# Seven products for batch 0's second expert layer, with partial sums begun in PSUM by ScalarE

## The chip, the cores and the metric

The kernel runs on one core of a Trainium2 chip. The metric is the device time of one execution in microseconds. Without the change it is 1115.46 us, the median of 3 runs (1114.99 to 1116.11). About 0.2% can be told from no change.

## The reference, cut to what matters

Three parts follow each other on 4 batches of 576 tokens: an attention over 32 memory slots, a two-layer network with a leaky activation, and a mixture of 4 experts. The change lies in the last part, which is

```
x: [2304, 512]   w1: [4, 512, 1024]   w2: [4, 1024, 512]
p = domain_probs / (sum of domain_probs over experts + 1e-9)
for e in range(4):
    h = max(x @ w1[e], 0)
    out += p[:, e:e+1] * (h @ w2[e])
```

## The kernel before, in words

**Arithmetic.** All matrices are kept transposed: features on the 128 partitions, tokens along the free dimension, 288 tokens (HB, half a batch) to a matmul. Operands are split into a high part (ScalarE casts to fp32r) and a low part (VectorE or GpSimd subtracts, `sub_to`, line 309); a product takes three passes, high x high, high x low, low x high. So one block product with an inner length of 256 is 2 x 3 = 6 matmuls of 128x128 by 128x288.

**Units.** The experts' 4 x 1024 hidden features are 8 groups g of 512. `plan_experts` (line 1112) walks through units (half, g, b): first batches 0 and 1 for all g, then batches 2 and 3 for all g. In a unit, each of two parts hp (256 hidden features) is an `Up` (line 875): the first product by Strassen's algorithm in Winograd's form, 7 block products p1 to p7 (42 matmuls) into three PSUM banks ux, uy, uw out of the six of ps_a. p2 adds onto p1's bank, p7 and p4 onto p6's, p3 onto p5's. v1 copies p1's sum to SBUF, and VectorE adds it: v16 = uy + v1 after p6, v167 = uy + v1 after p7, and c21, c22 and c12 add in the bank or to SBUF. Batches 0 and 1 ("banked") are gated straight out of the banks (max with 0, times p; line 950); batches 2 and 3 are first written to h and then gated in halves (`gate_half`, line 966).

**Second product.** It runs as a side stream, one block at a time between the Ups of the next unit, into two banks (ps_h). `Down` (line 998) is plain: 8 blocks of 12 matmuls. `Seven` (line 1038) does it with seven products in two halves: 14 blocks of 6 matmuls, 4 differences S of the gated hidden features, 7 high parts H, 7 low parts L. Batch 0 uses Down for all 8 groups; batches 1 to 3 use Seven for g = 0 to 6 and Down for g = 7. After each block D, a flush F takes it to an accumulator in SBUF: a ScalarE copy for g = 0, a VectorE addition later. At the end of a batch the seven accumulators are combined (cb) and Down's last blocks are added and stored.

**Weights.** w1's sums (ws), high (wh) and low parts (wl) and w2's quarters (vh, vl), their four sums (ss, sh, sl) are made in the first half, stored to HBM (wk, vk, sk) and read again in the second half (wr, cl, vr), all by DMAs issued from SP's queue. The tiles of w2 lie in a ring of 8 (ring2), and one more, wP4, lies in another pool.

**The order.** Each of these steps is a named task. The string ORDER (line 30) lists them in the order in which they are issued; each engine runs its own instructions in that order and waits by semaphores for the others. The set ON_VECTOR (line 254) names the low parts, differences and sums that VectorE does; the others go to GpSimd. Names are kind, g, b, then hp or a number: p6_320 is p6 of group 3, batch 2, part 0; D32_5 a block of the second product.

Of the kernel before, what the change touches and what calls it, by code (L numbers as in the profile page):

```python
# [100 lines left out]
p5_100 c12_011 ws11 p6_100 wh11 sk0S1 D01_4 F01_4 D01_0 F01_0 S01_4 H01_4 sh0S4 p5_110 S01_5 H01_3 rw22 D01_3 F01_3
D01_5 wl110 wl111 F01_5 rw23 ss1S1 v16_100 p2_100 vh110 vh111 sl0S4 sk0S2 vk010 sk0S4 L01_4 p7_100 H01_5 S01_6 H01_6
p5_101 v167_100 c11_100 c22_100 D01_8 D01_9 p5_111 F01_8 p3_100 c12_100 F01_9 p1_101 p4_100 c21_100 vh101 ss1S2 sh1S1
p6_101 v1_101 v16_101 vl110 D01_2 F01_2 L01_5 D01_11 sl1S1 p7_101 L01_6 F01_11 v167_101 wk11 p2_101 hi0_100 D01_10
L01_3 D01_12 F01_12 p4_101 rw14 F01_10 ss1S4 sh1S4 vl111 vk011 D01_13 F01_13 p1_110 c11_101 c22_101 p6_110 hi1_100
c21_101 hi1_101 lo1_100 p3_101 c12_101 D01_7 p1_111 v1_110 p2_110 v16_110 lo0_100 vl101 p7_110 c11_110 D01_6 v167_110
hi0_101 rw15 sl1S4 F01_6 p4_110 wk10 F01_7 lo0_101 vh100 lo1_101 D10_4 c22_110 p3_110 c21_110 H11_0 F10_4 c12_110
vl100 ss1S3 D10_7 vk111 L11_0 ws20 S11_1 H11_1 L11_1 sh1S3 F10_7 pg11 D10_6 F10_6 p6_111 v1_111 v16_111 D11_1 F11_1
D10_0 F10_0 p2_111 c11_111 p7_111 v167_111 c22_111 D10_1 wh20 wl201 rw24 sl1S3 F10_1 wl200 p4_111 c21_111 D10_5 F10_5
p3_111 ws21 c12_111 S11_4 S11_5 wh21 D10_2 F10_2 p1_200 v1_200 pg10 wl211 D10_3 H11_2 L11_2 sk1S4 p6_200 F10_3 p5_200  # L110
D11_3 H11_3 p2_200 rw25 ss2S1 v16_200 F11_3 L11_3 wl210 p7_200 v167_200 H11_4 D11_5 sk1S1 H11_5 sk1S3 c11_200 vh200
vl200 vk110 L11_4 S11_6 p6_201 p4_200 c21_200 p1_201 v1_201 sh1S2 D11_9 F11_5 F11_9 sl1S2 p1_210 D11_4 sh2S1 sl2S1
D11_2 p5_211 c22_200 p3_200 F11_2 F11_4 D11_8 c12_200 F11_8 D11_0 F11_0 v16_201 p2_201 ss2S2 sh2S2 sl2S2 p5_201 vh201
p7_201 c11_201 v167_201 c22_201 H11_6 vk200 L11_5 D11_11 F11_11 hi1_200 ss2S3 p6_211 lo1_200 D11_6 F11_6 p4_201 D11_7
F11_7 L11_6 vl201 hi0_200 lo0_200 p3_201 c21_201 c12_201 D11_10 v1_210 hi1_201 lo1_201 vk100 p6_210 v16_210 wk20 rw16
D11_13 F11_13 F11_10 p5_210 vh210 p7_210 v167_210 p2_210 c11_210 c22_210 p4_210 c21_210 D11_12 vh211 p3_210 c12_210
hi0_201 vl211 lo0_201 sk1S2 F11_12 H21_0 p1_211 vk211 sk2S1 vl210 D20_3 vk210 F20_3 D20_6 wk21 L21_0 S21_1 F20_6
v1_211 v16_211 sk2S2 D20_0 F20_0 p2_211 c11_211 ws30 wh30 p7_211 v167_211 wl301 D20_2 H21_1 c22_211 p3_211 c12_211
D20_4 F20_4 wl300 sh2S3 sl2S3 L21_1 ss2S4 F20_2 p4_211 c21_211 rw17 ws31 D20_1 F20_1 D20_5 F20_5 D20_7 sh2S4 D21_0
S21_4 p1_300 F20_7 H21_3 L21_3 wk30 F21_0 wh31 wl310 D21_3 D21_2 rw27 vh311 v1_300 p2_300 F21_3 H21_2 H21_4 wl311  # L120
sl2S4 S21_5 c11_300 p6_300 v16_300 D21_1 F21_1 p5_300 rw26 ss3S1 L21_4 H21_5 D21_6 F21_2 F21_6 sk2S4 L21_2 p7_300
p6_301 D21_8 D21_4 L21_5 F21_8 D21_5 v167_300 p4_300 S21_6 F21_4 H21_6 c22_300 p3_300 rw18 F21_5 c21_300 L21_6 c12_300
D21_7 vh310 wk31 sh3S1 vl310 vk310 p1_301 F21_7 v1_301 v16_301 hi0_300 D21_9 lo0_300 p2_301 F21_9 hi1_300 sl3S1 D21_10
p7_301 p1_310 p5_301 v167_301 c11_301 c22_301 vh301 F21_10 vh300 vl300 D21_11 F21_11 p3_301 vk300 vl311 c12_301
lo1_300 p4_301 D21_12 c21_301 F21_12 D21_13 p6_310 F21_13 v1_310 p2_310 v16_310 c11_310 vk311 ss3S2 ss3S4 p7_310
v167_310 vl301 hi0_301 lo0_301 ws40 p5_310 c22_310 p4_310 p3_310 c21_310 hi1_301 lo1_301 p1_311 H31_0 v1_311 D30_3
L31_0 c12_310 wh40 D30_5 wl400 F30_5 sh3S2 sl3S2 F30_3 p6_311 wl401 p2_311 D30_2 F30_2 D30_1 v16_311 F30_1 rw19 ws41
sh3S4 S31_1 D31_0 p5_311 p7_311 c11_311 v167_311 c22_311 D30_0 F30_0 H31_1 L31_1 F31_0 p3_311 p4_311 D31_1 pg20
c12_311 c21_311 F31_1 sk3S1 wh41 wl410 D30_4 ss3S3 F30_4 p1_400 S31_4 sk2S3 sl3S4 D30_7 p6_400 F30_7 v1_400 v16_400
D30_6 wl411 sk3S2 D31_2 H31_2 L31_2 p7_400 S31_5 H31_5 rw28 H31_4 F30_6 v167_400 sh3S3 sl3S3 rw29 ss4S1 ss4S2 p6_401  # L130
L31_4 S31_6 D31_5 sh4S1 L31_5 F31_5 p5_400 p2_400 D31_3 c11_400 c22_400 p4_400 F31_2 p3_400 c21_400 H31_3 vh410 F31_3
vh400 vl400 wk40 D31_4 p1_401 rw111 F31_4 sl4S1 sk4S1 p6_410 pg21 c12_400 v1_401 p2_401 v16_401 hi1_400 vl410 L31_3
p7_401 D31_11 p1_410 hi0_400 vh411 F31_11 D31_9 H31_6 L31_6 lo1_400 v167_401 D31_8 vl411 F31_8 p4_401 c21_401 F31_9
sk3S3 D31_10 p5_401 vh401 F31_10 c11_401 ss4S4 c22_401 hi1_401 p5_410 D31_6 F31_6 v1_410 p3_401 c12_401 D31_7 p6_411
p2_410 v16_410 p7_410 lo1_401 F31_7 vl401 D31_13 D31_12 p1_411 v167_410 p4_410 c11_410 c22_410 sh4S4 hi0_401 lo0_401
lo0_400 F31_12 sl4S4 c21_410 p3_410 ss4S3 wk41 D40_0 H41_0 F31_13 D40_4 F40_0 D40_3 v1_411 p2_411 rw110 c12_410
# [137 lines left out]
def memory_attention_experts(ctx: ExitStack, tc: tile.TileContext, phi, q, kv, w_in, w_out, w1, w2, alpha, dp, out):  # L274
# [1335 lines left out]
```

## Time and profile before

| | |
|---|---|
| median of 3 runs | 1115.46 us |
| the profiled execution | 1115.43 us |
| its span, first to last instruction | 1113.3 us |
| TensorE, VectorE, ScalarE, GpSimd busy | 1105.6, 806.9, 443.6, 605.0 us |

The span is shorter than the execution by what lies around the program. In the rows, PE is TensorE's matmul and PEld its weight load, DVE is VectorE, ACT is ScalarE, POOL is GpSimd, SP is the queue that issues the DMAs; L888 is line 888 of the kernel. TensorE's matmuls overlap, so that a duration (296 ns) is longer than the distance between two starts.

### The profile page before, as it was taken

How to read it: one execution, taken by the hardware profiler on the slowest of the kernel's cores; microseconds unless marked ns; L12 is line 12 of the kernel's file. 1: busy time of each engine (PE TensorE's matmuls, PEld its weight loads, DVE VectorE, ACT ScalarE, POOL GpSimd, SP SyncE). 2: the span in 40 equal slices, each digit the busy share in tenths (PEclk: the TensorE clock that was granted, in tenths of full speed). 3: DMA queues.
4: the chain of work that ended last, by engine and by line, in shares of the span. 5: the costliest groups of instructions: out<-in, count | busy, mean ns of one | idle time of the engine just before them, and what ended most of it. 6: DMA issues, size and time to landing. Idle time of an engine off the chain costs nothing.

```text
span 1113.3 us, 21930 instructions
## 1 busy us (share of the span) xinstructions
PE 1105.6 (99%) x8668; PEld 1071.8 (96%) x8668; DVE 806.9 (72%) x1570; ACT 443.6 (40%) x911; POOL 605.0 (54%) x487
## 2 busy tenths in 40 slices
PE   9999999999999999999999999999999999999998
PEld 8679999999999999999999999999999999999998
DVE  6987786767556767777877777846677777777786
ACT  5676654534444544333333234324522222223220
POOL 3666555522345587898788878774433333335500
PEclk9999999999999999999999999999999999999999
DMA  9930211211020427585557364686555554634702
GB/s 371 390 145 21 95 58 58 76 40 40 1 87 30 181 96 295 178 312 202 190 230 267 116 257 156 232 319 203 178 176 177 180 162 154 218 126 149 253 7 85
DMA packets 61046, 181.20 MB, mean 163 GB/s; under 512 B 6288, under 2 KB 23696, under 8 KB 57232
## 3 DMA queue, kind: packets, MB, share of 16 engines
q1 hardware_dynamic: 60944, 179.80, 45.2%
q8 instruction: 68, 1.11, 0.4%
q14 instruction: 34, 0.28, 0.1%
HBM read 115.52 MB, written 64.26 MB: 161 GB/s over the span
## 4 chain that ended last, share of the span: by engine, by line
PE 97%; DVE 2%; issue 0%; ACT 0%; POOL 0%; POOLq 0%; DVEq 0%
PE c L1083 20%; PE y L690 17%; PE uy L888 14%; PE o L1015 13%; PE uw L888 9%; PE ux L888 9%; PE h L656 9%; PE y L687 1%; PE pw L615 1%; PE warm L322 1%; PE pm L424 1%; PE h L653 1%; PE pc L456 0%; DVE w L309 0%; DVE h L1058 0%
## 5 line engine op out<-in xcount | busy, mean ns | idle before, releaser
L690 PE MATMUL y<-g,wout 128*128 128x288 f32 x1440 | 205.3, 296 | 0.0
L690 PEld LDWEIGHTS y<-g,wout 128*128 128x128 f32 x1440 | 195.3, 188 | 7.3 <-ACT g L675 2.5
L888 PE MATMUL uy<-x,w 128*128 128x288 f32 x1152 | 183.7, 296 | 0.0
L309 POOL TENSOR_TENSOR gc<-h,gc 128x576 fp32r<-128x576 f32 x78 | 117.6, 1514 | 119.5 <-ACT gc L1066 119.4
L888 PEld LDWEIGHTS uy<-x,w 128*128 128x128 f32 x1152 | 162.7, 188 | 0.7 <-DVE v L922 0.5
L1066 ACT CAST gc<-h 128x576 fp32r<-128x576 f32 x119 | 79.3, 675 | 196.6 <-DVE h L1058 121.5
L1083 PE MATMUL c<-gc,w2c 128*128 128x288 f32 x1008 | 155.0, 295 | 0.5 <-DVE acc2y L1101 0.5
L1083 PEld LDWEIGHTS c<-gc,w2c 128*128 128x128 f32 x1008 | 140.7, 188 | 0.8 <-DVE acc2y L1101 0.8
L309 POOL TENSOR_TENSOR g<-act,g 128x288 fp32r<-128x288 f32 x80 | 68.5, 864 | 125.5 <-ACT g L675 84.1
L888 PE MATMUL uw<-x,w 128*128 128x288 f32 x768 | 122.4, 296 | 0.2 <-DVE ux L922 0.2
L1015 PE MATMUL o<-g,w 128*128 128x288 f32 x864 | 122.4, 295 | 0.0
L888 PE MATMUL ux<-x,w 128*128 128x288 f32 x768 | 122.2, 295 | 0.0
L1015 PEld LDWEIGHTS o<-g,w 128*128 128x128 f32 x864 | 117.1, 188 | 0.0
L656 PE MATMUL h<-a,wp 128*128 128x288 f32 x720 | 110.2, 296 | 0.0
L671 DVE SCALAR_TENSOR_TENSOR act<-neg,bet,h 128x288 f32<-128x288 f32 x120 | 60.4, 510 | 67.9 <-ACT neg L662 62.2
L888 PEld LDWEIGHTS uw<-x,w 128*128 128x128 f32 x768 | 108.5, 188 | 0.5 <-DVE ux L922 0.4
L888 PEld LDWEIGHTS ux<-x,w 128*128 128x128 f32 x768 | 108.8, 188 | 0.0
L656 PEld LDWEIGHTS h<-a,wp 128*128 128x128 f32 x720 | 99.9, 188 | 5.7 <-issue 2.3
L662 ACT ACTIVATE neg<-h 128x288 f32<-128x288 f32 x128 | 52.2, 411 | 97.6 <-PE h L656 94.9
L1101 DVE TENSOR_TENSOR acc<-c,acc 128x288 f32<-128x288 f32 x144 | 64.9, 454 | 35.4 <-PE c L1083 33.3
L922 DVE TENSOR_TENSOR v<-uy,v 128x288 f32<-128x288 f32 x128 | 58.1, 454 | 40.2 <-PE uy L888 36.9
L675 ACT CAST g<-act 128x288 fp32r<-128x288 f32 x120 | 51.2, 433 | 43.7 <-DVE act L671 32.9
(195 smaller groups left out, 1832.9 us busy)
## 6 DMA issues: line engine op xcount, KB each, us to landing
kw<-w SPq DMA_DIRECT2D x16, 1792.0 KB, 8.9
raww<-in_w SPq DMA_DIRECT2D x32, 512.0 KB, 4.7
w<-kw SPq DMA_DIRECT2D x32, 512.0 KB, 4.8
kS<-sS SPq DMA_DIRECT2D x28, 512.0 KB, 5.8
w2c<-kS SPq DMA_DIRECT2D x28, 512.0 KB, 4.5
kw<-w SPq DMA_DIRECT2D x25, 512.0 KB, 5.5
w<-kw SPq DMA_DIRECT2D x48, 256.0 KB, 4.3
kv<-in_kv SPq DMA_DIRECT2D x8, 1152.0 KB, 12.3
```

What stands on the lines that cost most here:

```text
L309: eng.tensor_tensor(out=out, in0=in0, in1=in1.bitcast(F32), op=ALU.subtract)
L656: mm(p, wp_t[b, c, g][:, x, fs], a_t[b][:, y, g, o:o + HB], start=(n == 0), stop=(n == 5))
L662: nc.scalar.activation(out=self.neg, in_=self.p, func=AF.Relu, scale=-1.0)
L671: nc.vector.scalar_tensor_tensor(out=self.g, in0=self.neg, scalar=bet[:, ft:ft + 1], in1=self.p, op0=ALU.mult, op1=ALU.add)
L675: nc.scalar.copy(out=self.gt[:, 0, 0:HB], in_=self.g)
L690: mm(First.acc[d], w[:, x, d * 128:(d + 1) * 128], self.gt[:, y, 0:HB], start=(self.start and n == 0), stop=(self.stop and n == 2))
L888: mm(p, w[:, x, a, k], operand(self.b, i)[:, y, k], start=(start and n == 0), stop=(n == 5), skip_group_check=not start)
L922: nc.vector.tensor_tensor(out=out, in0=x, in1=y, op=ALU.add)
L1015: mm(p, w[:, x, i, d % 2 * 128:(d % 2 + 1) * 128], g, start=(m == 0), stop=(m == 11), skip_group_check=len(hps) == 1)
L1066: nc.scalar.copy(out=t[:, 0], in_=self.raw(q))
L1083: mm(p, w[:, x, i, m * 128:(m + 1) * 128], self.g_t[q][:, y, i], start=(k == 0), stop=(k == 5))
L1101: nc.vector.tensor_tensor(out=a, in0=self.ps[n], in1=a, op=ALU.add)
```

## The change

Batch 0 is done like batch 1: Seven for g = 0 to 6, Down for g = 7. In all Ups, v1 copies p1's sum from ux into the bank uy before p6, and p6, p7 and p4 add onto it; v16 and v167 become ScalarE copies of uy, and c21 is gated straight from uy. All batches are gated from the banks, so that the half gates go. For b < 2 and g > 0, every odd block n of Seven is "seeded": a new task E copies the accumulator into the block's bank on ScalarE, the product adds onto it, and the flush is a ScalarE copy. A first matmul with `start=True` in uy, whose result is overwritten by v1, is added to each p1 of group 0 and batch 0. c21's, v16's and v167's additions go.

The differences, the sums of w1 and w2 and the low parts of w2 can now be on either engine (`engine(...)`), and ON_VECTOR grows from 280 to 426 names. ring2 has 7 buffers for 8, the pool yt 9 for 6, and wP4 goes into ring2. The pieces of w2 are made at other places of a group's two units, and quarter (0, 1) is made for g = 7 alone. ORDER is new from its 1271st task on (the last tasks of the layer before); it has 4247 tasks for 4080.

The core of the diff, without ORDER and ON_VECTOR:

```diff
-        for name, key, bufs in (("w1b", ("w1", 1), 1), ("pp", "p", 2), ("hp", "h", 3), ("vp", "v", 1), ("ring2", "w2", 8), ("accp", "acc", 2), ("yt", "y", 6), ("xt", "xt", 2)):
+        for name, key, bufs in (("w1b", ("w1", 1), 1), ("pp", "p", 2), ("hp", "h", 3), ("vp", "v", 1), ("ring2", "w2", 7), ("accp", "acc", 2), ("yt", "y", 9), ("xt", "xt", 2)):
...
+        t = pools["w2"].tile([128, 2, 512], F32R, tag="w", name=f"w2c{g}{q}")
...
+    def seeded(g, b, n):
+        return g > 0 and b < 2 and n % 2 == 1
...
-            self.seven, self.hs = b > 0 and g < NG - 1, None
-            self.banked = b < 2
+            self.seven, self.hs = g < NG - 1, None
...
         def p1(self):
             self.x = self.bank("ux")
             self.product(self.x, A11, B11, True)
+            if (self.g, self.b) == (0, 0):
+                self.y = self.bank("uy")
+                w = w1_t[self.g, self.hp].rearrange("p x (c k n) -> p x c k n", c=7, k=2)
+                mm(self.y, w[:, 0, A11, 0], operand(self.b, B11)[:, 0, 0], start=True, stop=True)
 
         def p6(self):
-            self.y = self.bank("uy")
-            self.product(self.y, V2, T2, True)
+            self.product(self.y, V2, T2, False)
...
         def v1(self):
-            self.v1_t = self.v("v1")
-            nc.scalar.copy(out=self.v1_t, in_=self.x)
+            if (self.g, self.b) != (0, 0):
+                self.y = self.bank("uy")
+            nc.scalar.copy(out=self.y, in_=self.x)
 
         def v16(self):
             self.v16_t = self.v("v16")
-            self.add(self.v16_t, self.y, self.v1_t)
+            nc.scalar.copy(out=self.v16_t, in_=self.y)
...
         def c11(self):
-            if self.banked:
-                self.gated(0, 0, self.x)
-            else:
-                nc.scalar.copy(out=self.block(0, 0), in_=self.x)
+            self.gated(0, 0, self.x)
...
         def added(self, i, j, bank, x, y):
-            if self.banked:
-                self.add(bank, x, y)
-                self.gated(i, j, bank)
-            else:
-                self.add(self.block(i, j), x, y)
+            self.add(bank, x, y)
+            self.gated(i, j, bank)
...
         def v167(self):
             self.v167_t = self.v("v167")
-            self.add(self.v167_t, self.y, self.v1_t)
+            nc.scalar.copy(out=self.v167_t, in_=self.y)
...
         def c21(self):
-            self.added(1, 0, self.y, self.y, self.v1_t)
+            self.gated(1, 0, self.y)
...
-            if not self.late and q in (P1, P2, P4):
+            if n not in self.ps:
+                self.ps[n] = ps_h.tile([128, 512], F32, tag="h", name=f"c{self.name}{n}")[:, 0:HB]
+            p, fresh = self.ps[n], not seeded(self.g, self.b, n)
+            if self.b < 2 and q in (P1, P2, P4):
                 w = w2_t[(self.g,) + C_W[q]]
             else:
...
-                    mm(p, w[:, x, i, m * 128:(m + 1) * 128], self.g_t[q][:, y, i], start=(k == 0), stop=(k == 5))
+                    mm(p, w[:, x, i, m * 128:(m + 1) * 128], self.g_t[q][:, y, i], start=(fresh and k == 0), stop=(k == 5), skip_group_check=not fresh)
                     k += 1
+
+        def seed(self, n):
+            q, m = divmod(n, 2)
+            p = self.ps[n] = ps_h.tile([128, 512], F32, tag="h", name=f"c{self.name}{n}")[:, 0:HB]
+            nc.scalar.copy(out=p, in_=acc_t[self.b][q][:, m])
...
             a = acc_t[b][q][:, m]
-            if self.g == 0:
+            if self.g == 0 or seeded(self.g, b, n):
                 nc.scalar.copy(out=a, in_=self.ps[n])
             else:
                 nc.vector.tensor_tensor(out=a, in0=self.ps[n], in1=a, op=ALU.add)
...
+                if g == NG - 1:
+                    if t == 0:
+                        more.setdefault((1, 1), []).extend((do_w2, g, hp, 0) for hp in range(2))
+                        more.setdefault((1, 3), []).extend((do_w2, g, hp, 1) for hp in range(2))
+                else:
                     for place, fs in (
-                        ((1, 1), [(do_sum, g, "S1")]),
-                        ((1, 2), [(do_part, g, "S1", 0), (do_sum, g, "S2")]),
-                        ((1, 3), [(do_part, g, "S1", 1), (do_part, g, "S2", 0)]),
-                        ((1, 4), [(do_sum, g, "S4"), (do_part, g, "S2", 1)]),
+                        ((0, 3), [(do_w2, g, 0, 0)]),
+                        ((0, 4), [(do_sum, g, "S1")]),
+                        ((1, 0), [(do_part, g, "S1", 0), (do_sum, g, "S2")]),
+                        ((1, 1), [(do_w2, g, 1, 0), (do_part, g, "S1", 1)]),
+                        ((1, 2), [(do_sum, g, "S4"), (do_part, g, "S4", 0)]),
+                        ((1, 3), [(do_part, g, "S4", 1), (do_sum, g, "S3"), (do_raw, 4 * g + 4)]),
+                        ((1, 4), [(do_part, g, "S3", 0)]),
...
+                        ((0, 0), [(do_part, g, "S3", 1), (do_part, g, "S2", 0)]),
+                        ((0, 1), [(do_part, g, "S2", 1), (do_w2, g, 1, 1)]),
...
-                    loads = {-1: [(do_c_load, 0, q) for q in (P1, P5, P4)], 3: [(do_c_load, 0, q) for q in (P2, P3)], 7: [(do_c_load, 0, q) for q in (P7, P6)]}
+                    loads = {-1: [(do_c_load, 0, q) for q in (P1, P5, P4)], 7: [(do_c_load, 0, q) for q in (P2, P3, P7, P6)]}
...
+                more.setdefault((0, 4), []).extend((do_unspill, 2, i, j) for i, j in ((0, 0), (0, 1), (1, 1)))
...
                     do(f"D{old.g}{old.b}_{n}", old.product, n)
+                    if old_seven and n < 13 and seeded(old.g, old.b, n + 1):
+                        do(f"E{old.g}{old.b}_{n + 1}", old.seed, n + 1)
                     do(f"F{old.g}{old.b}_{n}", old.flush, n)
```

## Rows read from the trace of the kernel before

**Rows 1.** Busy time, share and instructions of each engine, whole span, from the page.

```profile
PE 1105.6 (99%) x8668; PEld 1071.8 (96%) x8668; DVE 806.9 (72%) x1570; ACT 443.6 (40%) x911; POOL 605.0 (54%) x487
```

**Rows 2.** Chain that ended last, shares of the span by engine, from the page.

```profile
PE 97%; DVE 2%; issue 0%; ACT 0%; POOL 0%; POOLq 0%; DVEq 0%
```

**Rows 3.** Stretches: start:end, length, busy (instructions) by engine, granted clock, DMA share, GB/s.

```profile
372.00:745.00 373.00, 372.41 (x2792) 370.88 (x2791) 278.07 (x524) 139.49 (x244) 298.87 (x227) 1.00 0.60 222
745.00:1110.00 365.00, 364.46 (x2747) 364.00 (x2745) 263.52 (x512) 104.89 (x201) 125.78 (x83) 1.00 0.48 160
812.00:1005.00 193.00, 193.00 (x1458) 193.00 (x1458) 145.78 (x296) 52.51 (x95) 64.21 (x43) 1.00 0.54 176
```

**Rows 4.** Groups by line, tile and shape: xcount, busy us, mean ns, idle before. Plain second product.

```profile
L1015 PE MATMUL o<-g,w 128*128 128x288 f32 x864 | 122.4, 295 | 0.0
...
L1015 PE MATMUL o<-g,w2l 128*128 128x288 f32 x192 | 26.1, 295 | 0.0
```

**Rows 5.** Timeline around one Up of batch 2: start us, duration us, engine, line.

```profile
905.27 0.96 PE L888 MATMUL ux<-x,w 128*128 128x288 f32 x6
...
905.94 0.85 PEld L1083 LDWEIGHTS c<-gc,w2c 128*128 128x128 f32 x6
906.07 0.95 PE L1083 MATMUL c<-gc,w2c 128*128 128x288 f32 x6
906.27 0.40 ACT L926 COPY v<-ux 128x288 f32<-128x288 f32 x1 [0.87 <-PE ux L888]
906.74 0.84 PEld L888 LDWEIGHTS uy<-x,w 128*128 128x128 f32 x6
906.86 0.95 PE L888 MATMUL uy<-x,w 128*128 128x288 f32 x6
```

**Rows 6.** Timeline where a sum v16 came late, first half; idle time in brackets.

```profile
416.04 2.88 DVE L309 TENSOR_TENSOR w<-s,w 128x1024 fp32r<-128x1024 f32 x1
...
418.21 0.86 PEld L888 LDWEIGHTS ux<-x,w 128*128 128x128 f32 x6
...
418.85 0.45 DVE L922 TENSOR_TENSOR v<-uy,v 128x288 f32<-128x288 f32 x1
...
419.35 0.83 PEld L888 LDWEIGHTS uy<-x,w 128*128 128x128 f32 x6 [0.28 <-DVE v L922]
```

**Rows 7.** Groups of VectorE in the first half, 372 to 745 us.

```profile
L922 DVE TENSOR_TENSOR v<-uy,v 128x288 f32<-128x288 f32 x66 | 29.9, 453 | 17.6 <-PE uy L888 14.9 <-ACT g L991 1.0 <-PE c L1083 0.8
...
L1032 DVE TENSOR_TENSOR acc<-o,acc 128x288 f32<-128x288 f32 x56 | 24.8, 453 | 21.1 <-PE o L1015 20.9
...
L309 DVE TENSOR_TENSOR gc<-h,gc 128x576 fp32r<-128x576 f32 x21 | 19.9, 950 | 3.0 <-ACT gc L1066 3.0
L309 DVE TENSOR_TENSOR w<-s,w 128x1024 fp32r<-128x1024 f32 x11 | 18.4, 1671 | 2.0 <-ACT w L793 2.0
L309 DVE TENSOR_TENSOR g<-h,g 128x576 fp32r<-128x576 f32 x14 | 16.6, 1183 | 1.7 <-ACT g L991 1.6
...
L309 DVE TENSOR_TENSOR sS<-S,sS 128x512 fp32r<-128x512 f32 x12 | 12.1, 1008 | 0.0
```

**Rows 8.** Groups of VectorE in the second half, 745 to 1110 us.

```profile
L968 DVE SCALAR_TENSOR_TENSOR c<-c,p 128x576 f32<-128x576 f32 x28 | 21.5, 767 | 1.8 <-ACT c L948 0.7
...
L309 DVE TENSOR_TENSOR gc<-h,gc 128x576 fp32r<-128x576 f32 x20 | 15.9, 797 | 0.0
```

**Rows 9.** Groups of ScalarE over the whole span.

```profile
L1066 ACT CAST gc<-h 128x576 fp32r<-128x576 f32 x119 | 79.3, 675 | 196.6 <-DVE h L1058 121.5 <-POOL h L1058 21.6 <-PE o L1015 12.8
...
L926 ACT COPY v<-ux 128x288 f32<-128x288 f32 x64 | 25.5, 398 | 65.1 <-PE ux L888 43.2 <-DVE uy L922 15.7 <-DVE uw L922 2.6
...
L1099 ACT COPY acc<-c 128x288 f32<-128x288 f32 x24 | 9.5, 402 | 12.1 <-PE c L1083 12.0
```

**Rows 10.** Transfers of w2's weights: xcount, size, median us from issue to landing.

```profile
w2c<-kw SPq DMA_DIRECT2D x14, 512.0 KB, 5.8
```

More of the change, by code (lines that the diff above doesn't have):

```diff
@@ L826, in s_sum @@
         x, y = (cs_t[g, i] if i in ("S1", "S2") else a[i] for i in (x, y))
-        nc.gpsimd.tensor_tensor(out=o, in0=x, in1=y, op=op)
+        engine(f"ss{g}{n}").tensor_tensor(out=o, in0=x, in1=y, op=op)
     def s_hi(g, n):
@@ L934, in open @@
                 return
-            if self.seven and self.hp and b_late(self.b):
-                if not c_raw:
-                    for j in range(2):
-                        c_raw[j] = rawp.tile([128, 1024], F32, tag="raw", name=f"c{j}")[:, 0:S].rearrange("p (i n) -> p i n", i=2)
-                self.hs = c_raw
-            else:
-                self.h = pools["h"].tile([128, 4, HB], F32, tag="h", name="h" + self.name)
-                self.hs = [self.h[:, 2 * j:2 * j + 2] for j in range(2)]
+            self.h = pools["h"].tile([128, 4, HB], F32, tag="h", name="h" + self.name)
+            self.hs = [self.h[:, 2 * j:2 * j + 2] for j in range(2)]
         def c11(self):
-            if self.banked:
-                self.gated(0, 0, self.x)
-            else:
-                nc.scalar.copy(out=self.block(0, 0), in_=self.x)
+            self.gated(0, 0, self.x)
         def gated(self, i, j, src):
@@ L1061, in hi @@
             k = self.slot[q]
[L1062 to L1065 removed]
+            c = self.b // 2, k // 2
+            if c not in c_slot:
+                c_slot[c] = unit(f"gc{c[0]}{c[1]}", F32R).rearrange("p (s x i n) -> p s x i n", s=2, x=2, i=2)
+            t = self.g_t[q] = c_slot[c][:, k % 2]
             nc.scalar.copy(out=t[:, 0], in_=self.raw(q))
@@ L1150, in do_w2 @@
             do(f"vl{g}{hp}{half}", w2_lo, g, hp, half)
-            if half:
+            if half and (g == NG - 1 or hp):
                 do_raw(4 * g + hp + 4)
@@ L1253, in plan_experts @@
                     loads = {2 * q + 1: [(do_w2_load, g, q % 2, q // 2)] for q in range(4)}
-            if (half, g, t) == (0, NG - 1, 1):
+            if (half, g) == (0, NG - 1):
                 for n, place in enumerate(((0, 0), (0, 0), (0, 1), (0, 1), (0, 2), (0, 2), (0, 3))):
-                    more.setdefault(place, []).append((do_combine, 1, n))
+                    more.setdefault(place, []).append((do_combine, b, n))
             if half and g == NG - 1:
@@ L1309, in plan_experts @@
                 c = Seven(g, b, n_seven, ups)
-                n_seven += b > 1
-                c.defer = not old_seven
+                n_seven += 1
+                c.defer = isinstance(old, Down)
             def s_do(x, *what):
@@ L1421, in plan_experts @@
             old = c if seven else Down(g, b)
-        do(f"gate0_{last.name}", last.gate, 0)
+            if (half, g, t) == (0, NG - 1, 1):
+                n_seven = 0
         for i in (1, 0):
```

457 lines of the change are left out of this document (207 added, 250 removed).

## The prediction

> **What bounds the kernel now.** I read the totals by engine first: TensorE is busy in 1105.6 of 1113.3 us, the next engine, VectorE, in 806.9 [rows 1]. A busy TensorE alone proves little, since matmuls overlap, so I went to the chain of waits: 97% of it is TensorE, 2% VectorE [rows 2]. Almost nothing stands between one matmul and the next; the kernel ends when TensorE has worked off its list. What can change the time is the number of matmuls, the spacing between them, and new gaps.
>
> The spacing comes from the busy times by stretch [rows 3]. From 812 to 1005 us (batches 2 and 3, one repeated pattern) 1458 matmuls start in 193.0 us: 132.4 ns each at a granted clock of 1.00, the 2.4 GHz level; six of them, one block product, start 0.79 to 0.80 us apart (905.27, 906.07, 906.86) [rows 5]. I use 132.2 ns. The experts' first half (batches 0 and 1, 372 to 745 us) starts 2792 in 373.0 us. At 132.2 ns they need 369.1, so 3.9 us are lost there today. The second half loses 365.0 - 2747 x 0.1322 = 1.8 us. There VectorE is busy 263.5 us, ScalarE 104.9; in the first half VectorE has 278.1 of 373.0, ScalarE 139.5, GpSimd 298.9.
>
> **Matmuls removed.** A plain second product of one batch and one 512-wide group is 8 output blocks of 12 matmuls, 96; by seven products it is 14 blocks of 6, 84. The rows agree: 864 + 192 = 1056 = 11 x 96 plain ones [rows 4]. The change turns batch 0's groups 0 to 6 from the one into the other: 7 x 12 = 84 fewer. It adds two, one in each p1 of group 0 and batch 0. Net 82 x 132.2 ns = **-10.84 us**, all of it on the path, as TensorE is the path.
> The rows give 132 ns per 288-column matmul. The Trainium skill (TensorE: Matmul & The Clock Gate, Part 1, on the 56 ns) puts warm matmuls N / 2.4 GHz + 2.5 ns apart, 122.5 ns here; by that the 82 would be worth 10.0 us. The measured spacing is longer and decides.
>
> **What the change puts on the other engines, first half.** I counted the tasks in the old and new order lists and in the list of tasks given to VectorE.
> - VectorE loses 96 bank sums (v16, v167 and c21's, 3 in each of 32 Ups), 53 accumulator additions (136 to 83) and 11 of batch 0's low parts. At 0.453 us for the first two and 1.183 for the last [rows 7]: -43.5 - 24.0 - 13.0 = -80 us.
> - It gains 43 low parts and 27 differences of the seven products, 11 sums and 10 low parts of w2 that were GpSimd's, 3 low parts of those sums, 6 low parts of w1. At 0.95 us for 576 columns, 1.01 for 512 and 1.67 or less for w1's [rows 7]: 66 + 24 + 10 = +100, and some 6 for sums of x, w1 and the accumulators. Net +26: 304 of some 365 us, 0.83 of the time against 0.75 now.
> - ScalarE gains 64 copies (v16, v167), 84 seeds E, 89 copies out of banks (22 to 111) at 0.40 each, and 49 high parts at 0.675 for 30 fewer old ones [rows 9]; 7 w2 casts go. +103 us: 0.66 of the time against 0.37.
> - GpSimd sheds about 75 us and is no danger.
> None of them reaches TensorE's load, so by load alone the change costs nothing. What counts is lateness: each engine works in order, and TensorE has two banks for the second product (ps_h) and six for the first (ps_a).
>
> **Chains that TensorE waits for.** TensorE works in order too, so what waits on it holds up everything behind it; a waiting seed or copy holds up ScalarE's later copies and high parts. Three kinds: p6 -> v16 -> p7 and p7 -> v167 -> p4 (the bank must be copied before it is added to), bank -> flush -> next product in that bank, and two new ones: p1 -> v1 -> p6, since v1 now writes the bank that p6 adds to, and flush -> seed E -> seeded product. I measured the cover of each as the TensorE work that the order list puts between its two ends.
> The trace shows how one block product covers one ScalarE copy [rows 5]: the p1 group starts at 905.27 and ends at 906.23, v1 runs from 906.27 for 0.40, and the load of the group after the next begins at 906.74, 0.07 us after the copy's end. A VectorE consumer hands over to TensorE within 0.05 us (419.30 to 419.35) [rows 6]. So an idle ScalarE just fits. When the engine is not idle, one sees [rows 6]: a 2.88 us stretch of w1's low part delays v16 to 418.85, and the p7 behind it starts 0.28 us late.
> First half: chains with one block product of cover or less grow from 19 to 33 (p6 to p7 2 to 7, p7 to p4 8 to 7, bank to product 9 to 19). p1 to p6 has at least two products of cover. Of 84 seeded products 20 have two products or less for flush plus seed, 0.46 + 0.40 plus handovers. That is 34 more tight chains. Lower end: none late, 0 us, or a gain, since a copy of 0.40 replaces an addition of 0.46 and GpSimd's load, which slows VectorE's two-input work (0.95 against 0.80 us [rows 7, 8]), falls; at best the 3.9 us lost now go. Upper end: all 34 late by that 0.28 [rows 6], 9.5 us. I take one in three, **+3.1 us**, nearer the lower end, because VectorE ran at 0.75 and GpSimd at 0.80 with 19 such chains and the whole loss was 3.9.
> Second half: 23 of 32 p1 to p6 have just one product of cover; 0.07 us were to spare with the copy going to SBUF, and ScalarE is free there: its last instruction before v1 is a high part issued two or more products earlier. A copy into a bank does not occur in the trace: between 0 and, if it took VectorE's 0.46 us, about 0.03 each, 0.7 in all. Against it VectorE loses the 56 half gates of 0.77 us [rows 8] and 64 + 32 sums, and gains 128 gates from banks at 0.46: about -30 us, so that some of the 1.8 us lost there may come back. Net **0**, bounds -1.8 and +0.7.
>
> **The turn between the halves.** ring2 has 7 buffers for 8, and wP4 joins them. On SP's queue the weights for group 0 now go P4, P5, P1, P3, P7, P2, P6; the last four must wait for batch 1's last plain products. From the end of the last of these to the product that uses P2's weights the order list has 6.4 us of TensorE work, where 5.8 us pass until such a load lands [rows 10]; behind it on SP stand the w1 reloads and P6's weights. 0 to 3 us; **+0.3**. In the steady pattern each of the seven loads still has about 20 us. The unspill loads sit in three more yt buffers and later in SP's queue; their first user is over 16 us away: 0. The pieces of w2 move to other places of a group's two units, 7 quarters fewer, with the same stores to HBM: 0. The first 372 us keep their order but for the last few blocks; the final sums are as before: 0.
>
> **Sum** against the profiled execution's 1115.43 us (0.03 under the median of 1115.46): 1115.43 - 10.84 + 3.1 + 0 + 0.3 = **1108.0 us**.
>
> **Rivals.** *Full gain.* No chain comes late, as in the second half now: 1115.43 - 10.84 = 1104.6, and 1102 if half of what the first half loses goes too. For it: 34 tight chains sit on engines that are never full. Against: VectorE's load rises where it already makes TensorE wait. Chance 0.20.
> *Slower: the seeds starve the banks.* With two banks, a seed must be written while the other bank's product runs, so each seeded product waits for flush, then seed: 0.46 + 0.40 plus 0.2 of handovers. If one VectorE instruction of 0.95 us stands ahead of the flush it is 2.0 us, against covers of 1.6 (20 of them) or 2.4 (21): 20 x 0.6 us plus the 34 chains late, 9.5, is 21.5, and 1126 us. It decides once VectorE runs about an instruction behind throughout the first half, which at 0.83 load it need not; at 0.95 it would. Chance 0.09.
> The Trainium skill (Perfetto Trace Analysis, Optimizing Tensor Performance) says that independent groups should rotate through different PSUM banks so that evacuation overlaps the next group's matmuls; a seed takes a bank out of that rotation early. By that rule the slower case has its place at the seeds; no seed stands in the trace yet.
> *Eaten up.* v16 and v167 have one buffer each, now written by ScalarE and read by VectorE's c12 and c22: a late VectorE stops ScalarE, and with it seeds, copies and high parts. If the tight chains come late by all of 9.5 us and the turn costs 1: 1115. Chance 0.09.
> Whether the banks really add to the seed is a matter of values, not of time.
>
> **How the numbers follow.** Forecast 0.62, full gain 0.20, slower 0.09, eaten up 0.09. The measurement can tell about 0.2%, 2.2 us: below 1113.2 is faster, above 1117.7 slower. Forecast and full gain lie below: faster 0.82, same 0.09, slower 0.09. The range goes from 1104.0 (most of the full gain) to 1113.5 (the 9.5 us end, without the slower case).
>
> **What would show it.** 5426 expert matmuls for 5508, and the total down by 82. In the second half still 132 ns per matmul, no idle time before uy's loads, v1's copy at 0.40 us or less. In the first half a loss of some 7 us against 369.1 - 10.8; its waits before c's loads should name ScalarE's seeds and VectorE's flushes, a few tenths each. Wrong: a repeated gap after each p1 in the second half, waits of over 0.5 us at the seeds, a gap of microseconds at the first products of group 0 of batch 2, or a matmul spacing other than 132 ns.

## The result and the profile after

The changed kernel takes 1102.93 us (median of 5 runs, 1102.66 to 1105.52), the kernel before beside it 1116.06 (1114.99 to 1116.11): a ratio of 0.9891, 95% interval 0.9877 to 0.9906. Two later sets of runs gave 1103.61 against 1115.56 (0.9897, 0.9884 to 0.9911) and 1103.01 against 1115.74 (0.9883, 0.9869 to 0.9896). So it is faster by 12 to 13 us. I had forecast 7.4, and the median lies below my whole range, 1104.0 to 1113.5.

The profiled executions went from 1115.43 to 1103.97 us, the spans from 1113.3 to 1102.2. The first lines of the page of the changed kernel, by engine [rows 1] and of the chain of waits [rows 2]:

```profile
PE 1094.0 (99%) x8586; PEld 1060.5 (96%) x8586; DVE 805.2 (73%) x1517; ACT 546.0 (50%) x1195; POOL 504.5 (46%) x413
```

```profile
PE 98%; DVE 1%; DMA 1%; issue 0%; SPq 0%; POOL 0%; ACT 0%; POOLq 0%; DVEq 0%
```

There are 82 matmuls fewer, and TensorE is still the path. The two halves of the experts, to be laid beside [rows 3] (same columns):

```profile
372.00:738.00 366.00, 365.37 (x2748) 364.44 (x2747) 295.12 (x487) 232.06 (x498) 230.28 (x172) 1.00 0.62 223
738.00:1099.00 361.00, 359.93 (x2712) 359.10 (x2711) 244.50 (x497) 113.62 (x227) 92.08 (x64) 1.00 0.52 165
```

By the measure of the prediction (length less 132.2 ns per matmul) the first half now loses 366.0 - 363.3 = 2.7 us against 3.9, and the second 361.0 - 358.5 = 2.5 against 1.8. The sum is -10.84 - 1.2 + 0.7 = -11.3; the spans differ by 11.1. The changed kernel was profiled again in the first of the two later sets, the first yardstick below:

```profile
372.00:738.00 366.00, 365.95 (x2756) 365.37 (x2755) 296.48 (x489) 231.38 (x497) 230.18 (x171) 1.00 0.61 224
738.00:1097.00 359.00, 357.74 (x2697) 357.07 (x2696) 242.74 (x493) 113.66 (x227) 91.44 (x63) 1.00 0.52 165
```

Here 1.7 and 2.5 us are lost, which makes -10.84 - 2.2 + 0.7 = -12.3; its span of 1100.9 us is 12.4 shorter than the old one. Which waits are left in the first profile, by the weight loads of TensorE from 372 to 1099 us (who waits <- for what: us in all, times, longest; the view lists waits of more than 0.15 us):

```profile
PEld c L1057 <- DVE h L951: 1.0, 1, 1.0
PEld ux L892 <- DVE uw L929: 0.8, 1, 0.8
PEld c L1057 <- DVE acc L1077: 0.4, 1, 0.4
PEld uw L892 <- DVE ux L929: 0.3, 1, 0.3
```

Four waits in all, and none names a seed (ACT c) or a copy v1, v16 or v167 (ACT uy, ACT v). The first and third stand at 1032 and 1034 us, where the waits of the matmuls name a load of w2 (DMA w2c): VectorE had been done by then. The loads of the helpers came out as counted: VectorE 295 us in the first half (I had 304 of 365), ScalarE 0.63 of the time (0.66), GpSimd down by 69 us (75). And yet none of the new chains stands among the waits. Smaller delays show from start to start, where 0.132 us is the rule. In the old kernel's first half 22 matmuls start more than 0.16 us behind the one before and lose 2.7 us together. In the new one it is 12 and 1.8 us, 0.8 of it at the turn to batch 2, and in the yardsticks, which have no wait at the turn, 8 starts and 0.9 us in one, 10 and 1.0 in the other. At the bank uy, which VectorE's sums v16 and v167 had to read before p7 and p4 could add to it and ScalarE's copies read now, such starts went from 8 to 1, at the banks of the seven-product blocks from 8 to 2; at uw there are 7 for 6.

How near they run is seen at the tightest of the 84 seeds, here in the timeline:

```profile
509.01 0.70 ACT L1075 COPY acc<-c 128x288 f32<-128x288 f32 x2 [1.52 <-PE c L1057]
509.46 1.22 PEld L1057 LDWEIGHTS c<-gc,sS 128*128 128x128 f32 x9
509.55 1.24 PE L1057 MATMUL c<-gc,sS 128*128 128x288 f32 x8
509.74 0.40 ACT L1063 COPY c<-acc 128x288 f32<-128x288 f32 x1
```

The seed ends at 510.14. The seeded product is the second in the group of eight matmuls and starts after six, at 510.36: 0.21 us later. I paired all 84 seeds with their products in the same way: the least margin is 0.21, the median 0.88 us.

### The profile page after: what moved, and what is told of

It reads as the page before. It is cut to its first block, busy times and chain, and to the rows that moved or that the text cites. A ratio compares the mean times of both kernels' runs of the same rounds, so it can differ in the third digit from the quotient of the medians.

```text
span 1102.2 us, 22022 instructions
## 1 busy us (share of the span) xinstructions
PE 1094.0 (99%) x8586; PEld 1060.5 (96%) x8586; DVE 805.2 (73%) x1517; ACT 546.0 (50%) x1195; POOL 504.5 (46%) x413
## 4 chain that ended last, share of the span: by engine, by line
PE 98%; DVE 1%; DMA 1%; issue 0%; SPq 0%; POOL 0%; ACT 0%; POOLq 0%; DVEq 0%
PE c L1057 28%; PE y L700 18%; PE uy L892 14%; PE ux L892 9%; PE uw L892 9%; PE h L666 9%; PE o L1003 5%; PE y L697 1%; PE warm L332 1%; PE pw L625 1%; PE pm L434 1%; PE h L663 1%; DMA w2c<-kS 1%; PE pc L466 0%; DVE h L1030 0%; PE pt L450 0%
## 5 line engine op out<-in xcount | busy, mean ns | idle before, releaser
L319 POOL TENSOR_TENSOR gc<-h,gc 128x576 fp32r<-128x576 f32 x91 | 135.5, 1494 | 202.4 <-ACT gc L1038 200.0
L1038 ACT CAST gc<-h 128x576 fp32r<-128x576 f32 x196 | 129.0, 674 | 113.0 <-DVE h L1030 85.4
L1057 PE MATMUL c<-gc,w2c 128*128 128x288 f32 x1176 | 182.9, 295 | 0.9 <-DMA w2c<-kS 0.9
L1057 PEld LDWEIGHTS c<-gc,w2c 128*128 128x128 f32 x1176 | 164.6, 188 | 1.5 <-DVE h L951 1.0
L1077 DVE TENSOR_TENSOR acc<-c,acc 128x288 f32<-128x288 f32 x252 | 112.0, 453 | 72.4 <-PE c L1057 71.8
L1057 PE MATMUL c<-gc,sS 128*128 128x288 f32 x672 | 102.7, 295 | 0.0
L319 DVE TENSOR_TENSOR gc<-h,gc 128x576 fp32r<-128x576 f32 x105 | 90.8, 871 | 12.3 <-ACT gc L1038 12.2
L1057 PEld LDWEIGHTS c<-gc,sS 128*128 128x128 f32 x672 | 93.4, 188 | 0.0
L1075 ACT COPY acc<-c 128x288 f32<-128x288 f32 x140 | 55.5, 401 | 58.5 <-PE c L1057 57.6
```

The source lines that it names most:

```text
L319: eng.tensor_tensor(out=out, in0=in0, in1=in1.bitcast(F32), op=ALU.subtract)
L1038: nc.scalar.copy(out=t[:, 0], in_=self.raw(q))
L1057: mm(p, w[:, x, i, m * 128:(m + 1) * 128], self.g_t[q][:, y, i], start=(fresh and k == 0), stop=(k == 5), skip_group_check=not fresh)
L1075: nc.scalar.copy(out=a, in_=self.ps[n])
L1077: nc.vector.tensor_tensor(out=a, in0=self.ps[n], in1=a, op=ALU.add)
```

## The experiments

My first theory was that the seeds and copies end in time and that VectorE's lower load is what keeps them in time; the rival, that they do come late as forecast, hidden by something else. The changed kernel is 1103.61 and 1103.01 us in the sets of runs that had it as yardstick; for the others I take 1103.2 (the kernel before was at 1115.4 to 1115.7 in each of these sets). The name in brackets is how a run is called further on.

**The matmuls put back (m84).**

```diff
+            if self.b == 0 and n % 2 == 0 and n:
+                for i in range(2):
+                    mm(p, w[:, 0, 0, m * 128:(m + 1) * 128], self.g_t[q][:, 0, 0], start=True, stop=True)
```

> The changed kernel once more, as the yardstick for the runs beside it. Every theory: 1102.9 us, a ratio of 0.988 to 0.990 to the kernel before.

> The changed kernel with 84 matmuls put back: in 6 of the 7 even blocks of each of batch 0's seven-product units two matmuls with start=True go ahead, whose sums the block's first matmul overwrites. Theory 1 (each removed matmul is worth its spacing of 132.5 ns, and what is left of the gain comes from waits that went away): 84 x 0.1325 = 11.1 us more, 1114.0, about 2 us under the kernel before. Rival (the whole gain of 13.1 us hangs on the 82 matmuls, 160 ns each): 13.4 us more, 1116.3, level with the kernel before. Rival (my forecast's tight chains do cost 3 us, and the added matmuls now cover them): less than 9 us more, under 1112.

Yardstick 1103.61 us; with the matmuls 1115.38 (1113.73 to 1120.75), ratio 0.9999 to the kernel before (0.9987 to 1.0011). So 11.8 us more, 0.7 over 84 spacings: by the time alone this lies between the 11.1 of my first theory and the 13.4 of the rival. The waits of its matmuls say where the rest is:

```profile
PE ux L892 <- DMA w<-kw: 1.5, 1, 1.5
...
PE c L1060 <- DMA w2c<-kS: 1.1, 2, 1.0
```

The first of them, at the turn of the halves, is not in the yardstick's profile, and the matmuls start 132 ns apart in both. So a matmul is worth its spacing, not 160 ns. All other parts of the change together, new chains included, come out within 1.5 us of nothing: this kernel has two matmuls more than the old one, and the old time.

**Seeds and copies undone (noseed, vec, both).**

```diff
-        return g > 0 and b < 2 and n % 2 == 1
+        return False
...
-            nc.scalar.copy(out=self.v16_t, in_=self.y)
+            nc.vector.tensor_copy(out=self.v16_t, in_=self.y)
...
-            nc.scalar.copy(out=self.v167_t, in_=self.y)
+            nc.vector.tensor_copy(out=self.v167_t, in_=self.y)
```

The first edit alone (the seed tasks leave the order with it), the other two alone, and all three:

> The changed kernel without seeds: the odd blocks of batches 0 and 1 start in an empty bank, and VectorE adds them to the accumulator in 0.453 us. VectorE goes from 295 to some 333 of 366 us in the first half (0.91), ScalarE from 232 to some 164. Theory 1 (the seeds are in time and cost nothing; they matter because they keep VectorE early): slower by 1 to 8 us, 1104 to 1111, with waits of TensorE that name VectorE. Rival (the seeded chains come late, as my forecast had it, and other things hide that): faster by up to 2 us, 1101 or so.

> The changed kernel with the 128 copies v16 and v167 done by VectorE and not by ScalarE. VectorE gets 64 x 0.45 = 29 us in each half: 324 of 366 us in the first (0.89), 274 of 361 in the second (0.76). Theory 1 (what counts is whether VectorE is early): the first half gets 1 to 4 us slower, the second none, 1104 to 1107. Rival (the copies' engine is of no matter, since the bank and not the engine is what TensorE waits for): no difference, 1102.9.

> The changed kernel without seeds and with v16 and v167 copied by VectorE: the seven products for batch 0 without the relief of VectorE. VectorE would have 295 + 38 + 29 = 362 of 366 us in the first half (0.99). Theory 1: VectorE now sets the end of the first half; 10 us or more are lost, 1113 or above, so that the 82 matmuls bring nothing. Rival (VectorE's load is not what decides): the sum of the two edits alone, under 1108.

1139.62 us (+36.0), 1131.61 (+28.4) and 1167.31 (+64.1): the first two far over what my first theory gave (8 and 4 us at most), the third over its floor of 1113 by 54. Without seeds 36 of the 38 us put on VectorE are lost, with the copies on VectorE 28 of the 29 in the first half, with both 64 of 67. From 760 to 1000 us the copies cost a single wait of 1.3 us. VectorE was not full: without seeds it was busy 328 of the 398 us from 372 to 770.

```profile
372.00:770.00 398.00, 374.13 (x2724) 365.57 (x2723) 328.23 (x568) 175.19 (x332) 233.63 (x171) 0.99 0.55 200
```

It and TensorE wait for each other (TensorE's matmuls first, then VectorE from 440 to 620 us, both without seeds):

```profile
PE c L1053 <- DVE acc L1073: 14.8, 19, 2.0
```

```profile
DVE acc L1073 <- PE c L1053: 27.2, 27, 1.9
```

In the changed kernel VectorE's flushes wait for products too, 14.6 us in this stretch, but there no matmul waits for them. Without seeds a flush waits for its product, the low parts behind it start late, and the next flush, behind those, holds up TensorE, as here:

```profile
508.11 0.94 DVE L315 TENSOR_TENSOR gc<-h,gc 128x576 fp32r<-128x576 f32 x1
508.98 0.44 DVE L1073 TENSOR_TENSOR acc<-c,acc 128x288 f32<-128x288 f32 x1
509.48 0.82 PEld L1053 LDWEIGHTS c<-gc,w 128*128 128x128 f32 x6 [1.76 <-DVE acc L1073]
```

So in this order the change rests on ScalarE doing these flushes and copies. The order was left as it is made for seeds, so these numbers are what the parts are worth in this order, not in one made without them.

**The same load at other places (ldup, nspool).**

```diff
-            sub_to(eng, t[:, 1], self.raw(q), t[:, 0])
+            for _ in range(2 if eng is nc.vector and self.b < 2 and q not in (P1, P6, P4) else 1):
+                sub_to(eng, t[:, 1], self.raw(q), t[:, 0])
```

and, in the kernel without seeds, ahead of that `sub_to`,

```diff
+            if self.b < 2 and q not in (P1, P6, P4):
+                eng = nc.gpsimd
```

> The changed kernel with 40 of the 72 low parts that VectorE makes for batches 0 and 1 made twice (0.913 us each): 37 us more on VectorE in the first half, as much as without seeds (38 us), but at places where no bank waits for it. Theory 1 (VectorE's list runs in step with TensorE's, so that every microsecond put on it anywhere is lost, as 36 of 38 without seeds and 28 of 29 with the copies on VectorE): 30 us or more, 1133 and above. Theory 2 (only what stands between a product and the next use of its bank counts): under 10 us more, below 1113.

> The kernel without seeds, with 40 low parts of batches 0 and 1 moved from VectorE to GpSimd: VectorE back at some 297 us in the first half, GpSimd at some 292, as before the change. Theory 1 (VectorE's load decides): most of the 36 us come back, 1105 to 1115. Theory 2 (the flushes stand at places of the order where VectorE has no room, whatever its load): 1125 or above.

(The traces count 36 added low parts, 33 us, and 36 moved ones; my counts had taken in names that don't occur.) 1127.53 us (+24.3): between the two theories, 24 of 33 us lost where no bank is flushed (its matmuls wait 5.9 us for flushes and 3.8 for low parts). And 1158.71 (+55.5): with VectorE's load taken back to where it was the kernel gets slower still, and TensorE waits for flushes as it did without seeds (14.8 us):

```profile
372.00:770.00 398.00, 363.62 (x2596) 352.90 (x2595) 293.24 (x511) 167.17 (x318) 271.49 (x202) 0.98 0.53 193
```

```profile
PE c L1055 <- DVE acc L1075: 14.1, 17, 2.3
```

The move has a price of its own: the low parts take 1.6 us on GpSimd, and 4.3 us of the matmuls' waits name GpSimd and 7.5 ScalarE, so that this run alone would not rule out load. Together the two speak against load alone and against the banks alone. What was left is the place: an instruction added anywhere delays what stands behind it on its engine, up to the next idle time. In the second kernel the granted clock fell too; its TensorE timeline after a wait of 2.67 us:

```profile
701.02 1.81 PE L888 MATMUL uw<-x,w 128*128 128x288 f32 x6 [2.67 <-DVE ux L925]
702.63 1.64 PE L1055 MATMUL c<-gc,w 128*128 128x288 f32 x6
704.07 3.08 PE L1055 MATMUL c<-gc,sS 128*128 128x288 f32 x12
```

From 702.63 to 704.07 six matmuls take 1.44 us, 240 ns each, the 1.2 GHz level. Its mean clock is 0.991, which makes 0.009 x 1157 = 10 of its 55 us (an estimate; its two runs at 0.996 and 0.998 took 1152 us); without seeds 0.996, 5 of 36.

**More work for GpSimd (pdup).** The first edit of the pair above with `nc.gpsimd` in place of `nc.vector`, for all its low parts.

> The changed kernel with the 26 low parts that GpSimd makes for batches 0 and 1 made twice (1.58 us each): 41 us more on GpSimd in the first half, 271 of 366. In the trace VectorE's instructions on SBUF alone take 0.75 us for 576 columns when GpSimd is idle and 1.0 to 1.3 when it works; those with a bank among their operands take 0.45 either way. They are 172 of VectorE's 366 us. Theory 1 (GpSimd's work costs time through VectorE): 41 x 0.47 = 19 us more of overlap, a quarter to a third of it lost, 5 to 6 us, 1107 to 1110. Rival (GpSimd has time to spare and nothing comes of it): under 1 us.

1129.44 us (+26.2), five times what I expected, though GpSimd was idle for over a third of the first half. (It was given 34 low parts, not 26: 34 x 1.58 = 54 us.) VectorE, with nothing added, is busy 324.3 us (485 instructions, 372 to 762 us) for 295.1 (487):

```profile
372.00:762.00 390.00, 374.67 (x2737) 368.38 (x2736) 324.34 (x485) 231.60 (x497) 295.57 (x205) 0.99 0.57 207
```

Three of its groups (changed kernel, 372 to 738 us; then this one, 372 to 768 us):

```profile
L319 DVE TENSOR_TENSOR gc<-h,gc 128x576 fp32r<-128x576 f32 x64 | 58.0, 913 | 5.2 <-ACT gc L1038 5.1
L1077 DVE TENSOR_TENSOR acc<-c,acc 128x288 f32<-128x288 f32 x84 | 37.7, 452 | 21.3 <-PE c L1057 21.0
L319 DVE TENSOR_TENSOR w<-s,w 128x1024 fp32r<-128x1024 f32 x15 | 20.0, 1331 | 0.0
```

```profile
L319 DVE TENSOR_TENSOR gc<-h,gc 128x576 fp32r<-128x576 f32 x64 | 68.7, 1081 | 7.8 <-ACT gc L1038 7.6
L1078 DVE TENSOR_TENSOR acc<-c,acc 128x288 f32<-128x288 f32 x84 | 37.6, 451 | 18.6 <-PE c L1058 18.2
L319 DVE TENSOR_TENSOR w<-s,w 128x1024 fp32r<-128x1024 f32 x15 | 24.4, 1628 | 0.0
```

The low parts, on SBUF alone, go from 913 to 1081 ns, w1's of 1024 columns from 1331 to 1628; the flushes, with a bank among their operands, stay at 452. Beside that GpSimd itself is late, by the waits of the matmuls:

```profile
PE c L1058 <- POOL gc L319: 10.3, 11, 2.4
```

**The place in the order alone (swap).** 24 of VectorE's 84 flushes in the first half go behind the next low part or difference of VectorE, as here in the order:

```diff
-D20_11 p7_300 F20_8 wl310 D20_12 wk30
+D20_11 p7_300 wl310 F20_8 D20_12 wk30
```

> The changed kernel as yardstick for the two runs beside it: 1102.9 to 1103.6 us.

> The changed kernel with 24 of VectorE's flushes of batches 0 and 1 moved behind the next low part or difference that VectorE makes (0.7 to 1.6 us); nothing else changes, and every engine has the same work. Theory 2 (what counts is the place in the order): each of the 24 banks comes free about 1 us later, where a seed or a product waits with a few tenths to spare: 24 x 0.3 to 0.7 us, 7 to 17 us more, 1110 to 1120. Theory 1 (load decides, place does not): under 1 us, 1103 to 1104.

1109.44 us against 1103.01: +6.4, 0.27 per flush moved, just under the 7 I gave as the least, and far from nothing. No engine has more to do. Same stretch, this kernel and the changed one:

```profile
372.00:745.00 373.00, 369.39 (x2758) 366.19 (x2757) 295.99 (x490) 231.56 (x498) 231.04 (x172) 1.00 0.60 219
```

```profile
372.00:745.00 373.00, 372.37 (x2801) 371.44 (x2800) 300.46 (x497) 234.29 (x502) 232.75 (x174) 1.00 0.62 224
```

The helpers are busy as before, within 5 us, and TensorE starts 43 matmuls less. The waits are the two that my forecast was afraid of, flush and seed:

```profile
PEld c L1057 <- DVE acc L1077: 3.3, 7, 0.8
PEld c L1057 <- ACT c L1063: 2.5, 4, 0.9
```

**Seeds and v1 doubled (seed2, v1x2).**

```diff
-            nc.scalar.copy(out=p, in_=acc_t[self.b][q][:, m])
+            for _ in range(2):
+                nc.scalar.copy(out=p, in_=acc_t[self.b][q][:, m])
```

and likewise v1's copy for batches 2 and 3.

> The changed kernel with each of the 84 seeds written twice by ScalarE: 0.41 us more between flush and product, ScalarE at 266 of 366 us in the first half (0.73). In the trace of the changed kernel the seed ends 0.21 us (least), 0.44 (lowest tenth), 0.88 (median) before the product's first matmul; 4 of 84 end less than 0.40 before it. Theory 1 (slack): those 4 come late by 0.2 us at most, with a few knock-on waits 0.5 to 3 us in all, 1103.4 to 1106. Rival (the 20 chains with two products of cover or less stand at their limit): 20 x 0.4 = 8 us or more, 1111 and above.

> The changed kernel with v1 copied twice into the bank for batches 2 and 3. In the trace 23 of 32 of these copies end 0.208 us before p6's first matmul, and p6's first weight load begins some 0.14 earlier, so about 0.07 us are to spare. Theory 1: 23 x (0.38 - 0.07) = 7.1 us more, all in the second half, 1110.0. Rival (there is more room than the trace lets see, since the next product could go ahead or the first write into the bank waits later): under 3 us. Rival (second copies also delay ScalarE's other work): over 9 us.

Doubled seeds: 1107.90 us, +4.7 of the 34 us that ScalarE got: more than the 3 that slack allowed, less than the rival's 8. Of the three helpers ScalarE passes on the least of its added work in the first half. Doubled v1: 1111.75, +8.6 where I had 7.1. The waits in the second half, 745 to 1020 us, are as clean as a count:

```profile
PEld uy L892 <- ACT uy L935: 7.6, 23, 0.3
```

23 times 0.33 us of idle time before p6's weight load, where I had computed 0.31. What p6's matmuls lose is seen in its timeline:

```profile
897.72 0.95 PE L1058 MATMUL c<-gc,w2c 128*128 128x288 f32 x6
898.77 1.07 PE L892 MATMUL uy<-x,w 128*128 128x288 f32 x6
```

p6 starts 1.05 us behind the group before it, not 0.79, and takes 0.11 longer than that group, as its second matmul is late too: 23 x (0.26 + 0.11) = 8.5. The second copy takes 0.42 us more, so that some 0.05 were to spare, near the 0.07 that I had.

**Three loads and a store moved.** From here on the kernel itself is improved: three tasks of the order, then a fourth, change places.

```diff
-p2_630 wr700 p6_630
+p2_630 cl63 cl65 cl64 wr700 p6_630
...
-L62_3 cl63 p5_630
+L62_3 p5_630
...
-v16_631 cl65 L63_0 S63_1 wr702 D62_4 cl64 H63_1
+v16_631 L63_0 S63_1 wr702 D62_4 H63_1
...
-lo0_700 us300
+lo0_700 wk71 us300
...
-v167_710 wk71 F61_11
+v167_710 F61_11
```

> The changed kernel with three tasks moved in the order: the loads of w2's parts P3, P6 and P7 of group 6 (cl63, cl65, cl64) stand ahead of the first w1 reload of group 7 (wr700) on SP's queue and not behind it. The trace shows 1.4 us of TensorE waits at 1028 to 1034 us for these loads, issued at 1023.9, 1025.2 and 1027.9, after SP had waited until 1020.9 for the w1 buffer. Theory 1: those waits go, 0.5 to 1.4 us faster than the changed kernel beside it, 1101.5 to 1102.4. Rival (in most executions the loads are in time): no difference, 1102.9. Rival (the w1 reload is then late for group 7): slower by some tenths, with waits before the first products of group 7.

> The changed kernel with the three loads moved as before, and the store of w1's last part (wk71, 1.8 MB) moved ahead of the loads us300 on SP's queue, which then stands still from 682 to 697 us. The trace shows that store issued at 703 us between the w1 reloads of group 0, of which the first lands after 6.8 us and holds up p1 of batch 2 by 0.65 us (0.78 in the changed kernel's profile, 1.71 with the 84 matmuls put back). Theory 1 (the store takes the reloads' bandwidth): that wait goes, 0.3 to 0.8 us under the kernel with the three loads moved alone, about 1101. Rival (the reload is late for another reason): no difference, 1101.9.

> The kernel with the three loads and the store moved, once more beside the changed kernel on one chip: 1101.1, 1.5 to 2.5 us under the changed kernel, if both waits seen in the traces (0.7 and 1.9 us) stand in most executions; level with it, if they are of single executions.

The three loads alone: 1101.89 us against 1103.61 beside it. With the store too: 1101.09 (ratio to the kernel before 0.9873, 0.9859 to 0.9886) and again 1101.47 (0.9868, 0.9853 to 0.9883) against 1103.01 beside it. Its eight runs lie between 1100.88 and 1102.00, the changed kernel's thirteen at 1102.42 and above. The SP queue of the second yardstick and of the new kernel beside it:

```profile
1005.94 0.32 SPq L859 DMA_DIRECT2D w2l<-kw  x1
1020.25 2.94 SPq L822 DMA_DIRECT2D w<-kw  x2
1023.24 0.59 SPq L854 DMA_DIRECT2D w2c<-kS  x1
```

```profile
1005.79 0.32 SPq L859 DMA_DIRECT2D w2l<-kw  x1
1009.76 7.47 SPq L854 DMA_DIRECT2D w2c<-kS  x3
```

The queue stood still for 14 us behind a w1 load whose buffer TensorE was still reading, with w2's loads behind it:

```profile
SPq L822 <- PE ux L892: 13.9, 1, 13.9
```

Ahead of it the three are issued between 1009.8 and 1017.2, so that they could have gone earlier, and the waits for them, present in the profiles of the changed kernel, both yardsticks, m84, swap, seed2 and v1x2, are in none of the three with the new order. What the store brings is not settled: the wait at the turn stands in the profiles of the changed kernel (0.8 us), of m84 and of the kernel with the three loads moved, and is missing in seven others, two of them with the store moved.

## Why the prediction was wrong, step by step

**Right.** The path and the 82 matmuls: 10.84 us by their spacing, borne out by m84. The shorter 122.5 ns of the Trainium skill (TensorE: Matmul & The Clock Gate, Part 1) would make 84 of them 10.3 us; measured were 11.8, of which the rows put 11.1 on the spacing. The loads of the engines. The second half's chains at 0: v1 takes 0.38 us and leaves some 0.05, and v1x2 shows that this margin is real and not more. The rows I named as signs there (132 ns, no idle time before uy's loads) came true; those for the first half, a loss of some 7 us and waits that name seeds, did not.

**The step that failed** is the first half's "I take one in three, +3.1 us" for 34 new tight chains. Measured is a gain of 1.2 us in the changed kernel's profile (2.2 in the yardstick's: 366.0 - 2756 x 0.1322 = 1.7 lost). Where the new chains lie, at uy and at the banks of the seven-product blocks, matmuls that start late went from 16, 2.0 us together, to 3, 0.3 us. I had counted how many products lie between the ends of a chain, and then taken a share of late ones from one event [rows 6] and from the busy shares. Neither says whether a given chain is late. That depends on what stands ahead of it on its engine at that place, as swap shows at equal loads: 24 flushes moved by one instruction cost 6.4 us, twice my whole term. The old kernel's late v16 [rows 6] was such a place too: a 2.88 us instruction ahead of it, not a full engine. My lower end did name "a gain" of up to 3.9 us, but the range was cut at 1104.0, inside the case "full gain" (1102 to 1104.6), which happened and to which I gave 0.20.

**Sized wrong:** what VectorE gains when GpSimd does less. I let it stand as a remark for the lower end; by the 1024-column low parts it is 1671 ns [rows 7] before and 20.0 us / 15 = 1331 after (1628 in pdup, with GpSimd back at 296 us), by all of them 304 less 295 = 9 us.

**The turn** at +0.3: 0.8 us in one profile of the changed kernel, nothing in both yardsticks, and at w1's reload or a bank, not at P2's weights. **Not foreseen:** w2's loads of group 6 behind w1's on SP's queue, 1.4 to 1.9 us in the second half, where I had put these loads at nothing ("each of the seven loads still has about 20 us").

**The rival "the seeds starve the banks"** (1126) named the place at which the altered kernels lose, a bank that waits for its flush, with the wrong condition. I had it decide when VectorE runs at 0.95; the kernel without seeds, where flushes are late, lost 36 us at 0.82 (328 of 398 us), and in swap flushes and seeds came late at a load that had not changed. The page Perfetto Trace Analysis of the Trainium skill (Identifying the Most-Contended Engine) takes the engine with the highest occupancy to be optimized first. Here TensorE is that engine, and it is the path; for the helpers the runs speak against reading spare time from occupancy: GpSimd at 0.63 of the time lost 26 us for 54 us of work, ScalarE at the same 0.63 lost 5 for 34.

The late starts show where the first half got faster. The runs don't show which part of the 1 to 2 us beyond 10.84 is VectorE's relief and which is the new places of the order: the two came together, and undoing one upsets the other.

## What to carry to other kernels

Where engines work through fixed lists, a busy share is no measure of spare time: go to each tight chain, write down what stands ahead of it on its engine by measured durations, and only then call it late. A microsecond on a helper at 0.63 to 0.8 may cost nearly a microsecond, half of one or a seventh, so test with work added to one helper at a time. And look at queues that stand still: a load whose buffer is in use holds up those behind it that could go.

## What the hardware showed beyond what I expected

- GpSimd's work slows VectorE's instructions on SBUF by much more than I thought: 65 us more of GpSimd (296 for 230, its 34 added low parts and what they slow) made VectorE 29 us longer, in the instructions without a bank operand (low parts of 576 columns: 804 ns in the changed kernel's second half, where GpSimd is busy for a quarter of the time, 913 in its first, 1081 in pdup). A mean hides two kinds: of the 64 in the changed kernel's first half, the 30 with no GpSimd work beside them take 741 to 759 ns, the other 34 up to 1898. The page SBUF — State Buffer of the Trainium skill (Summary: rules for kernel authors) says that with two SBUF inputs on VectorE and a GpSimd operation that reads SBUF the second one to issue blocks until the first is done. The kinds affected agree, and so does the longest, 1.1 us over the 750 ns of an undisturbed one, within GpSimd's 1.58 us.
- A wait of TensorE costs more than its length: behind a late matmul the next one is 0.10 to 0.11 us late too (23 times in v1x2).
- Where TensorE waited for microseconds, the granted clock fell to the 1.2 GHz level for some matmuls (0.83 from 700 to 720 us, in the kernel without seeds and with low parts moved to GpSimd), which adds to what the waits cost.
